# One attention and two gated layers on one core: fewer output transfers, another order of the first loads, and small matmuls and copies moved

## The chip, the cores and the metric

The kernel runs on one core of a Trainium2 chip. The metric is the time of one execution on the device in microseconds (us); lower is better. The five engines of the core are named as the profile names them: PE multiplies matrices (PEld is its weight load), DVE, ACT and POOL work on vectors, and SP issues transfers.

## The reference

Three stages follow one another. All are float32 in and out.

```python
batch, n_heads, seq, head_dim = (4, 8, 576, 64);  n_pack = 32
p_packed = sm_attn(p, k, v)                 # 32 packed queries per head look at 576 keys
out      = sm_attn(q, p_packed, p_packed)   # 576 queries per head look at the 32 packed rows
x = out.transpose(0, 2, 1, 3).reshape(2304, 512)

h = x @ w_in                                # w_in 512 x 2048
x = (max(h, 0) + log1p(exp(-abs(h)))) @ w_out          # w_out 2048 x 512

gate = 1 / (1 + exp(-(x @ w_gate)))         # w_gate, w_val 512 x 1536
y = (gate * (x @ w_val)) @ w_out2           # w_out2 1536 x 512
```

`sm_attn` is softmax attention with a scale of 1/8. The softmax of each row takes its own maximum off and divides by its sum.

## The kernel before

**Attention.** The work is cut into eight units: four batches, and in each two groups `g` of four heads (`attn_unit`, L330). A unit loads k, q and v as tiles of 128 partitions by 1152 numbers, 576 KB each. It goes through these steps:

- PE turns the unit's p (L333, out of `pall`, where the p of all units lies) and, in nine turns of 128x128, its k (L313); ACT copies the results out of PSUM as `pT` and `kT`.
- Eight small matmuls, `scores` (L326), make the first scores. DVE takes the maximum (L345), ACT the exponential with the sum (L348), DVE the reciprocal (L353) and the scaling of the 128x576 weights (L354), and turns them (L357).
- 72 small matmuls (L369) multiply the weights with v into two PSUM banks `pp`. Eight copies of 64x32 (L377, through the helper's L96 on ACT and L98 on DVE) bring the packed rows into `ppT`. `PPA = [1, 0]` puts the first four copies on ACT and the last four on DVE.
- Eight more `scores` matmuls give the scores of the 576 queries against the packed rows. A second softmax follows on DVE, ACT and POOL (L391 to L409), and its weights are split into a high and a low part `A2h` and `A2l` (L410, L411).

The trace counts each small float32 matmul twice: 8 of the program are x16 there, and 72 are x144.

**First layer.** The packed rows are multiplied into the first layer's weights ahead of time: `prep_wp` (L468) makes `Wp` out of `ppT` and a block of `w_in` (L480, eight small matmuls for one batch). `emit_h` (L498) multiplies `Wp` with the split softmax weights in three passes (L113 to L115), ACT makes the softplus (L509 to L511), and `emit_out1` (L528) multiplies with `w_out` (L537 to L540). All weights come in as pairs of 32-bit words that DVE turns into float32 with three instructions per half block (`convert`, L189, L194, L198).

**Second layer.** `emit_gv` (L786) makes gate and value by seven products (L113 to L115) and sums; `emit_out2` (L853) multiplies with the last weights (L859 to L861), adds into `acc` (L867), and after the last block sends each tile of 128 rows out.

**Loads.** SP issues nearly all transfers from one queue, in the order in which the scheduler put them, and stands at one that must wait. `load_kqv` (L229) takes k, q and v tiles in a fixed order and puts each in a free place: a slice of the big accumulator `xa`, or one of `NEXT = 2` own tiles. For units 6 and 7 only two slices and the own tiles are left. `done_kqv` (L240) loads two more when a tile has been used. `load_next` (L144) loads the next weight block into one of two `raw` buffers. `convert` calls it again at its end, so that a weight block is loaded when an earlier one has been converted. The p of all units is loaded by two transfers that ACT issues at the start (L275): each has 1024 runs of 256 bytes.

Each transfer holds one of eight semaphores for transfers until it has landed, and the next transfer with the same semaphore waits for it at issue.

**Order.** A scheduler orders the instructions of each engine by priority, which follows the order of the program, and by when it thinks that their inputs are there. Nothing in the kernel sets a priority. Semaphores are added afterwards; each engine runs its own list in order.

**Output.** `emit_out2` sends a tile of 128 rows as four transfers of 32 rows, 64 KB each (L875), because the rows of one tile belong to blocks that lie apart in the output.

```python
    while a < e:
        b, r = divmod(a, S)
        ee, cc = divmod(r // NR, NC)
        nc.sync.dma_start(outv[b, ee, cc], acc[a - t0 : a - t0 + NR])
        a += NR
```

Line numbers in the text are those of this kernel. The changed kernel's lines lie a few further on.

Of the kernel before, what the change touches and what calls it, by code (L numbers as in the profile page):

```python
# [11 lines left out]
I32 = mybir.dt.int32  # L12
AF = mybir.ActivationFunctionType
ALU = mybir.AluOpType
# [6 lines left out]
def attn_moe_moe_kernel(  # L21
# [24 lines left out]
    nc = tc.nc  # L46
    B, H, S, D = q.shape
    NK = p.shape[2]
    NT, DM = out.shape
    F1 = w_in.shape[1]  # L50
    F2 = w_gate.shape[1]
    P = 128
    NR = 32
    NC = S // NR // 2
# [4 lines left out]
    KD = DM // P  # L59
# [8 lines left out]
    L0 = 3  # L68
    GP = 7
    PO = ['k0', 'q0', 'k1', 'v0', 'q1', 'v1']  # L70
    XR = 0
    EARLY = [0]
    NCV = 5
    SC = float(D) ** -0.5
# [11 lines left out]
    xa = cst.tile([P, KD * NT], F32, name="xa")  # L86
# [4 lines left out]
    def bank1():  # L91
        return ps_o[-1].tile([P, 512], F32, tag="o", name="ps1")
# [26 lines left out]
    att = tc.alloc_tile_pool(name="att", bufs=1, side="right")  # L119
# [14 lines left out]
    for c in range(NCH1):  # L134
        order += [("in", c, f) for f in range(2)] + [("out", c, f) for f in range(2)]
        if c > ECS:
            n = -(-len(early) // (NCH1 - c))
# [6 lines left out]
    def load_next():  # L144
        if not waiting:
            return
        nm, c, f = key = waiting.popleft()
        if XR and key == ("out", 0, 0):

            t = xa[:, : 2 * DM].bitcast(I32).rearrange("p (n t) -> p n t", t=2)  # L150
        else:
            t = raw.tile([P, KD * P, 2], I32, tag="raw", name="raw_" + nm)
        a = c * CF + f * P
        if nm in ("out", "o2"):
            nc.sync.dma_start(t.rearrange("p n t -> p (n t)"), w32[nm][a : a + P, :])
        elif nm == "in":

            for g in range(2):
                nc.sync.dma_start(
                    t[64 * g : 64 * g + 64].rearrange("p (k n) t -> p k (n t)", k=KD),  # L160
                    w32[nm][256 * g : 256 * g + 256, 2 * a : 2 * (a + P)].rearrange(
                        "(k p) x -> p k x", p=64
                    ),
                )
        else:
            nc.sync.dma_start(
                t.rearrange("p (k n) t -> p k (n t)", k=KD),
                w32[nm][:, 2 * a : 2 * (a + P)].rearrange("(k p) x -> p k x", p=P),
            )
        raws[key] = t  # L170
# [41 lines left out]


    KQV = 2 * NC * D
    NEXT = 2
    own = [att.tile([P, KQV], F32, name=f"own{i}") for i in range(NEXT)]
    plan = deque((nm, u) for u in range(2 * B) for nm in "kqv")
    first = sorted((plan.popleft() for _ in range(6)), key=lambda x: PO.index(x[0] + str(x[1])))
# [47 lines left out]
    ppT = ph1.tile([P, B, H, NK], F32, name="ppT")  # L266
# [4 lines left out]


    pall = att.tile([P, 2 * B, 2, D], F32, name="pall")
    for i in range(2):
        nc.scalar.dma_start(  # L275
            pall[:, :, i], p.rearrange("b (g h) n d -> (h n) (b g) d", g=2)
        )

    NWORK = 7
    SPL = []  # L280
# [14 lines left out]
    LEFT = 1  # L295
    MARGIN = 0
    G0 = 2
    PPA = [1, 0]
    NW = 3
    GAP = 2  # L300
    LATE = 2
# [17 lines left out]

    def scores(lhsT, xT, to):  # L320

        for e in range(2):
            r = slice(64 * e, 64 * e + 64)
            for h in range(4):
                n = slice(NK * h, NK * h + NK)
                nc.tensor.matmul(  # L326
                    to[e][n], lhsT(r, h), xT[r, :, n], start=True, stop=True
                )

    def attn_unit(u):  # L330
        b, g = divmod(u, 2)
        px = bank1()
        nc.tensor.transpose(px[:, :P], pall[:, u].rearrange("p i d -> p (i d)"), ident)  # L333
        pT = att.tile([P, P], F32, tag="pT", bufs=2, name="pT")
        nc.scalar.activation(pT, px[:, :P], AF.Copy)
        kT = att.tile([P, NC, P], F32, tag="kT", bufs=1, name="kT")
        yield from turned(kqv.pop(("k", u)), kT)
        done_kqv("k", u)
        s1 = bank2()
        scores(  # L340
            lambda r, h: pT[r, NK * h : NK * h + NK], kT,
            [s1[:, e, :HS].rearrange("p (c r) -> p c r", r=NR) for e in range(2)],
        )
        mx = att.tile([P, 4], F32, tag="mx", bufs=2, name="mx")
        nc.vector.tensor_reduce(mx[:, 0:1], s1[:, :, :HS], op=ALU.max, axis=AX.XY)  # L345
        nc.vector.tensor_scalar(mx[:, 1:2], mx[:, 0:1], -SC, None, op0=ALU.mult)
        a1 = att.tile([P, S], F32, tag="a1", bufs=1, name="a1")
        nc.scalar.activation(  # L348
            a1.rearrange("p (a t) -> p a t", a=2), s1[:, :, :HS], AF.Exp,
            bias=mx[:, 1:2], scale=SC, accum_out=mx[:, 2:3],  # L350
        )
        nc.vector.tensor_scalar(mx[:, 2:3], mx[:, 2:3], 1e-9, None, op0=ALU.add)
        nc.vector.reciprocal(mx[:, 3:4], mx[:, 2:3])  # L353
        nc.vector.tensor_scalar(a1, a1, mx[:, 3:4], None, op0=ALU.mult)  # L354

        a1T = att.tile([P, 2 * NC, NK], F32, tag="a1T", bufs=2, name="a1T")
        nc.vector.transpose(a1T.rearrange("p c n -> p (c n)"), a1)  # L357
        yield
        qT = att.tile([P, NC, P], F32, tag="qT", bufs=2, name="qT")
        yield from turned(kqv.pop(("q", u)), qT)  # L360
        done_kqv("q", u)
        vt = kqv.pop(("v", u)).rearrange("p (c e d) -> p c e d", c=NC, e=2)

        pp = [bank1() for _ in range(2)]
        for e in range(2):
            for c in range(NC):
                for h in range(4):
                    r = slice(NR * h, NR * h + NR)
                    nc.tensor.matmul(  # L369
                        pp[h // 2][64 * (h % 2) : 64 * (h % 2) + 64, :NK],  # L370
                        vt[r, c, e, :], a1T[r, e * NC + c, :],
                        start=e == c == 0, stop=(e, c) == (1, NC - 1),
                    )
        done_kqv("v", u)
        for h in range(4):
            for x in range(2):
                copy(  # L377
                    PPA[h // 2], ppT[64 * x : 64 * x + 64, b, 4 * g + h, :],
                    pp[h // 2][64 * (h % 2) : 64 * (h % 2) + 64, :NK],
                )  # L380
        yield
        s2 = [bank1() for _ in range(2)]
        scores(
            lambda r, h: ppT[r, b, 4 * g + h, :], qT,
            [x[:, :HS].rearrange("p (c r) -> p c r", r=NR) for x in s2],
        )

        a2 = att.tile([P, 2 * NC, NK], F32, tag="a2", bufs=3, name="a2")
        m2 = att.tile([P, 2, 2 * NC], F32, tag="m2", bufs=3, name="m2")
        for e in range(2):  # L390
            nc.vector.transpose(  # L391
                a2[:, e * NC : (e + 1) * NC].rearrange("p c n -> p (c n)"), s2[e][:, :HS]
            )
        nc.vector.tensor_reduce(m2[:, 0], a2, op=ALU.max, axis=AX.X)
        nc.vector.tensor_tensor(
            a2, a2, m2[:, 0].unsqueeze(2).to_broadcast([P, 2 * NC, NK]), op=ALU.subtract
        )
        nc.scalar.activation(a2, a2, AF.Exp, scale=SC)
        yield
        nc.vector.tensor_reduce(m2[:, 1], a2, op=ALU.add, axis=AX.X)  # L400
        nc.vector.tensor_scalar(m2[:, 1], m2[:, 1], 1e-9, None, op0=ALU.add)
        nc.vector.reciprocal(m2[:, 1], m2[:, 1])
        nc.gpsimd.tensor_tensor(
            a2, a2, m2[:, 1].unsqueeze(2).to_broadcast([P, 2 * NC, NK]), op=ALU.mult
        )
        yield

        A2 = att.tile([P, S], F32, tag="A2", bufs=2, name="A2")
        nc.vector.transpose(A2, a2.rearrange("p c n -> p (c n)"))  # L409
        nc.scalar.activation(A2h[b][:, g], A2, AF.Copy)  # L410
        split_lo(nc.gpsimd, A2l[b][:, g], A2, A2h[b][:, g])  # L411
        yield
# [36 lines left out]
    w_in_f, wo_hl, Wp = {}, {}, {}  # L449
# [18 lines left out]
    def prep_wp(items):  # L468

        n = len(items)  # L470
# [2 lines left out]
            for y in "hl"  # L473
        )
        ps = [bank1().rearrange("p (i n) -> p i n", i=2)[:, :n] for _ in range(2)]
        for i, (b, c) in enumerate(items):
            for h in range(4):
                for t in range(2):
                    r = slice(64 * t, 64 * t + 64)
                    nc.tensor.matmul(  # L480
                        ps[t][NK * h : NK * h + NK, i], ppT[r, b, 4 * t + h, :],
                        w_in_f[c][r, h, :], start=True, stop=True,
                    )
            Wp[b, c] = (hi[:, i], lo[:, i])
        for t in range(2):
            if n == 1 or items[0][0] == items[1][0]:
# [207 lines left out]
    load_kqv(6)  # L694
    for _ in range(2):
        load_next()
    units.extend(range(2 * B))
    n = 0
    jobs.append(("win0", prep_win(0)))
# [153 lines left out]
    def emit_out2(ps, c, t):  # L853
# [15 lines left out]
        if c == NCH2 - 1:  # L869
            t0 = ps * HB * S + t * P  # L870
            a, e = t0, t0 + P
            while a < e:
                b, r = divmod(a, S)
                ee, cc = divmod(r // NR, NC)
                nc.sync.dma_start(outv[b, ee, cc], acc[a - t0 : a - t0 + NR])  # L875
                a += NR

    spread = [0.0]
    steps = [(ps, f) for ps in range(2) for f in range(NF)]
# [60 lines left out]
```

## Time and profile before

| | |
|---|---|
| three runs, median (range) | 885.8 us (882.84 to 887.54) |
| the profiled execution: its own time | 884.71 us |
| its span, first to last instruction | 882.9 us |
| mean granted clock of TensorE | 0.977 |
| busy share: PE, PEld | 93%, 86% |
| busy share: DVE, ACT, POOL | 71%, 43%, 51% |
| chain that ended last: PE, DVE | 77%, 11% |
| chain that ended last: ACT, transfers, issue, POOL | 3%, 3%, 3%, 2% |

The span runs from the first to the last instruction; the execution's own time is 1.8 us longer. PE is the engine that sets the pace: it is busy for 823.5 of the 882.9 us. The profile cuts the span into 40 slices of 22 us, and PE is at 9 tenths or more in nearly all of them but the first four and the last. The granted clock is that of the slices in tenths of full speed, where full is 2.4 GHz and half is 1.2 GHz.

### The profile page before, as it was taken

The page shows a single profiled execution, that of the slowest core. Times are in us where ns is not written, and L with a number is a line of the kernel's source. Part 1 is how long each engine was busy: PE and PEld are TensorE (multiplying, and loading weights), DVE is VectorE, ACT ScalarE, POOL GpSimd, SP SyncE. Part 2 cuts the span into 40 slices and gives each one's busy share as a digit, 9 for nine tenths or more (in the row PEclk, how much of TensorE's full clock was granted, in tenths as well). Part 3 has the DMA queues.
Part 4 walks back from the last instruction along what each step waited for, and adds up shares of the span by engine and source line. Part 5 has one row for each costly group of instructions (what it writes and reads, how often), then busy time and mean ns, then how long its engine had stood idle before and what let it go on. Part 6 is the DMA issues. An engine that isn't in the chain of part 4 may idle for free.

```text
span 882.9 us, 17370 instructions
## 1 busy us (share of the span) xinstructions
PE 823.5 (93%) x7040; PEld 755.4 (86%) x7040; DVE 626.0 (71%) x1057; ACT 376.3 (43%) x659; POOL 451.9 (51%) x420
## 2 busy tenths in 40 slices
PE   2976999999999999998999999999989999999995
PEld 1655788889989999998989999999869999999984
DVE  0757676778686577558898688897898656766763
ACT  1453666466555556666633331232342432322210
POOL 0043232366473555576469687886883633634400
PEclk9787999999999999998999999999999999999998
DMA  8644030123152223100055454645435312213004
GB/s 266 220 139 122 28 110 29 31 67 97 39 172 60 49 70 110 43 25 1 1 170 177 155 168 150 186 129 157 139 87 141 86 48 71 79 44 95 13 1 107
DMA packets 52480, 85.67 MB, mean 97 GB/s; under 512 B 6960, under 2 KB 30640, under 8 KB 52400
## 3 DMA queue, kind: packets, MB, share of 16 engines
q1 hardware_dynamic: 50320, 84.04, 32.5%
q8 instruction: 55, 0.90, 0.4%
q10 hardware_dynamic: 2080, 0.52, 0.3%
q14 instruction: 25, 0.20, 0.1%
HBM read 65.67 MB, written 18.87 MB: 96 GB/s over the span
## 4 chain that ended last, share of the span: by engine, by line
PE 77%; DVE 11%; ACT 3%; DMA 3%; issue 3%; POOL 2%; SPq 0%; POOLq 0%; ACTq 0%; DVEq 0%
PE bank L115 9%; PE bank L113 9%; PE bank L114 9%; PE ps L537 6%; PE ps L540 6%; PE ps L538 6%; PE ps L861 5%; PE ps L859 5%; PE ps L860 5%; PE ps L115 3%; PE ps L114 3%; PE ps L113 3%; DMA pall<-in_p_dram 2%; PE ps L369 2%; PE ps L313 2%
## 5 line engine op out<-in xcount | busy, mean ns | idle before, releaser
L113 PE MATMUL bank<-aop,BH 128*128 128x288 f32 x672 | 198.8, 296 | 3.7 <-DVE work L824 1.5
L114 PE MATMUL bank<-aop,BH 128*128 128x288 f32 x672 | 197.9, 295 | 1.0 <-DVE aop L101 0.9
L115 PE MATMUL bank<-aop,BL 128*128 128x288 f32 x672 | 198.6, 296 | 0.0
L101 POOL TENSOR_TENSOR ghl<-g,ghl 128x576 fp32r<-128x576 f32 x64 | 93.8, 1469 | 133.5 <-ACT ghl L108 133.5
L537 PE MATMUL ps<-ghl,woh 128*128 128x288 f32 x512 | 148.7, 305 | 6.0 <-DVE xa L545 3.6
L538 PE MATMUL ps<-ghl,wol 128*128 128x288 f32 x512 | 144.6, 297 | 0.0
L545 DVE TENSOR_TENSOR xa<-xa,ps 128x288 f32<-128x288 f32 x224 | 97.2, 448 | 59.0 <-PE ps L540 58.0
L113 PEld LDWEIGHTS bank<-aop,BH 128*128 128x128 f32 x672 | 126.2, 188 | 9.1 <-issue 1.4
L114 PEld LDWEIGHTS bank<-aop,BH 128*128 128x128 f32 x672 | 126.4, 188 | 5.1 <-DVE aop L101 1.6
L115 PEld LDWEIGHTS bank<-aop,BL 128*128 128x128 f32 x672 | 126.5, 188 | 0.0
L101 POOL TENSOR_TENSOR BL<-cv,BH 128x512 fp32r<-128x512 f32 (+1 forms) x96 | 116.8, 1231 | 11.3 <-ACT BH L108 10.2
L537 PEld LDWEIGHTS ps<-ghl,woh 128*128 128x128 f32 x512 | 97.4, 190 | 15.9 <-DVE xa L545 6.2
L540 PE MATMUL ps<-ghl,woh 128*128 128x288 f32 x512 | 110.6, 297 | 0.1
L538 PEld LDWEIGHTS ps<-ghl,wol 128*128 128x128 f32 x512 | 97.5, 190 | 0.5 <-issue 0.5
L812 DVE TENSOR_TENSOR work<-work,bank 128x576 f32<-128x576 f32 (+1 forms) x100 | 70.8, 725 | 29.8 <-PE bank L115 29.4
L859 PE MATMUL ps<-oh,gv 128*128 128x512 f32 x216 | 84.6, 392 | 1.3 <-DVE xa L867 0.8
L860 PE MATMUL ps<-ol,gv 128*128 128x512 f32 x216 | 84.8, 393 | 0.0
L861 PE MATMUL ps<-oh,gv 128*128 128x512 f32 x216 | 84.7, 393 | 0.0
L113 PE MATMUL ps<-A2h,wph 128*128 128x288 f32 x256 | 78.6, 309 | 6.3 <-ACT A2h L410 2.7
L540 PEld LDWEIGHTS ps<-ghl,woh 128*128 128x128 f32 x512 | 83.1, 189 | 0.4 <-POOL ghl L101 0.4
L867 DVE TENSOR_TENSOR xa<-xa,ps 128x512 f32<-128x512 f32 x90 | 61.5, 684 | 27.4 <-PE ps L861 26.9
L114 PE MATMUL ps<-A2l,wph 128*128 128x288 f32 x256 | 77.7, 304 | 1.9 <-POOL A2l L101 1.9
(115 smaller groups left out, 1576.0 us busy)
## 6 DMA issues: line engine op xcount, KB each, us to landing
cv<-B SPq DMA_DIRECT2D x52, 256.0 KB, 2.7
B<-cv SPq DMA_DIRECT2D x48, 256.0 KB, 4.2
raw_in<-in_moe_w_in_dram SPq DMA_DIRECT2D x32, 256.0 KB, 4.1
raw_out<-in_moe_w_out_dram SPq DMA_DIRECT2D x16, 512.0 KB, 3.7
raw_g<-in_moe_w_gate_dram SPq DMA_DIRECT2D x12, 512.0 KB, 4.0
raw_v<-in_moe_w_val_dram SPq DMA_DIRECT2D x12, 512.0 KB, 4.4
raw_o<-in_moe_w_out_dram SPq DMA_DIRECT2D x12, 512.0 KB, 4.2
out_dram<-xa SPq DMA_DIRECT2D x72, 64.0 KB, 1.7
```

The lines of the kernel that those rows point to most:

```text
L101: eng.tensor_tensor(lo, x, hi.bitcast(F32), op=ALU.subtract)
L113: nc.tensor.matmul(ps, wh, xh, start=first, stop=False)
L114: nc.tensor.matmul(ps, wh, xl, start=False, stop=False)
L115: nc.tensor.matmul(ps, wl, xh, start=False, stop=last)
L537: nc.tensor.matmul(out_, wh[:, ms], gh[:, f], start=f == 0, stop=False)
L538: nc.tensor.matmul(out_, wl[:, ms], gh[:, f], start=False, stop=False)
L540: nc.tensor.matmul(out_, wo_hl[c, f][0][:, ms], gl[:, f], start=False, stop=f == 1)
L545: nc.vector.tensor_tensor(dst, dst, out_, op=ALU.add)
L812: nc.vector.tensor_tensor(to, x, y, op=ALU.add)
L859: nc.tensor.matmul(bank, gh[:, ts_], oh, start=f == 0, stop=False)
L860: nc.tensor.matmul(bank, gh[:, ts_], ol, start=False, stop=False)
L861: nc.tensor.matmul(bank, gl[:, ts_], oh, start=False, stop=f == 1)
```

## The change

It has seven parts.

1. A tile's output rows that lie one after the other in `outv` go out in one transfer of up to four blocks of 32 rows; a half of the tokens takes 12 transfers instead of 36.
2. The p of units 0 and 1 is loaded by four small transfers that ACT issues first (128 runs of 256 bytes each); that of units 2 to 7 by two transfers on SP's queue, after the first four of `w_in`.
3. The first two blocks of `w_out` get tiles of their own (`raw_first`), and are loaded at the start too.
4. To make room for these, k, q and v have one own tile instead of two (`NEXT = 1`).
5. The blocks of small matmuls (`scores`, the product with v, and those of `prep_wp`) are put 300 places ahead in priority.
6. All eight copies into `ppT` run on ACT.
7. The scaling of the first softmax's weights runs on ACT instead of DVE.

```diff
-    XR = 0
+    FIRST = [("out", 0, 0), ("out", 0, 1)]
...
-        if XR and key == ("out", 0, 0):
-
-            t = xa[:, : 2 * DM].bitcast(I32).rearrange("p (n t) -> p n t", t=2)
+        if key in FIRST:
+            t = att.tile([P, KD * P, 2], I32, name=f"raw_first{c}{f}")
...
-    NEXT = 2
+    NEXT = 1
...
-    for i in range(2):
-        nc.scalar.dma_start(
-            pall[:, :, i], p.rearrange("b (g h) n d -> (h n) (b g) d", g=2)
-        )
+
+    def load_p(eng, a, e):
+        src = p.rearrange("b (g h) n d -> (h n) (b g) d", g=2)
+        for i in range(2):
+            eng.dma_start(pall[:, a:e, i], src[:, a:e])
+
+    load_p(nc.scalar, 0, 1)
+    load_p(nc.scalar, 1, 2)
...
-    PPA = [1, 0]
+    PRIO = 300
...
     def scores(lhsT, xT, to):
-        for e in range(2):
...
+        with tc.high_priority(PRIO):
+            for e in range(2):
...
-        nc.vector.tensor_scalar(a1, a1, mx[:, 3:4], None, op0=ALU.mult)
+        nc.scalar.activation(a1, a1, AF.Copy, scale=mx[:, 3:4])
...
-                    PPA[h // 2], ppT[64 * x : 64 * x + 64, b, 4 * g + h, :],
+                    True, ppT[64 * x : 64 * x + 64, b, 4 * g + h, :],
...
     load_kqv(6)
+    for _ in range(2):
+        load_next()
+    load_p(nc.sync, 2, 2 * B)
     for _ in range(2):
         load_next()
...
                 ee, cc = divmod(r // NR, NC)
-                nc.sync.dma_start(outv[b, ee, cc], acc[a - t0 : a - t0 + NR])
-                a += NR
+                n = min((e - a) // NR, NC - cc)
+                nc.sync.dma_start(outv[b, ee, cc : cc + n], acc[a - t0 : a - t0 + n * NR])
+                a += n * NR
```

The product with v and the matmuls of `prep_wp` are put under the same `tc.high_priority(PRIO)` as `scores`.

The change moves instructions at three places that matter below.

SP's queue from its start, before (k, q and v go to `xa` or `own`, `raw_in` is a half block of `w_in`, `raw_out` one of `w_out`):

```order
L236 DMA xa<-in_k_dram 128x1152
L236 DMA xa<-in_q_dram 128x1152
L236 DMA xa<-in_k_dram 128x1152
L236 DMA xa<-in_v_dram 128x1152
L236 DMA xa<-in_q_dram 128x1152
L236 DMA xa<-in_v_dram 128x1152
L159 DMA raw_in<-in_moe_w_in_dram 64x4x256 x4
L236 DMA xa<-in_k_dram 128x1152
L236 DMA xa<-in_q_dram 128x1152
L155 DMA raw_out<-in_moe_w_out_dram 128x1024 x2
```

and with the change, from the same place:

```order
L235 DMA xa<-in_v_dram 128x1152
L158 DMA raw_in<-in_moe_w_in_dram 64x4x256 x4
L277 DMA pall<-in_p_dram 128x6x64 x2
L154 DMA raw_first_120<-in_moe_w_out_dram 128x1024
L154 DMA raw_first_122<-in_moe_w_out_dram 128x1024
L235 DMA xa<-in_k_dram 128x1152
L235 DMA xa<-in_q_dram 128x1152
L158 DMA raw_in<-in_moe_w_in_dram 64x4x256 x4
```

The first six transfers are the same. Then the rest of p and both halves of the first `w_out` block come ahead of unit 2's k and q, and the second block of `w_in` follows right behind them; before, it came as the eighteenth row, behind `raw_out` and nine tiles of k, q and v.

PE from its start, with the change (`kT` of unit 0 is `ps_129` to `ps_139`; `ps_149` is the first piece of unit 1's k):

```order
L337 MATMUL ps_124<-ident,pall 128x128
L316 MATMUL ps_129<-ident,xa 128x128 x3
L316 MATMUL ps_134<-ident,xa 128x128 x3
L316 MATMUL ps_139<-ident,xa 128x128 x3
L337 MATMUL ps_144<-ident,pall 128x128
L316 MATMUL ps_149<-ident,xa 128x128 x2
L330 MATMUL ps_158<-kT,pT 32x288 x8
```

Unit 0's first scores (the last row) stand behind the turn of unit 1's p and two turns of unit 1's k. Before, the same seven rows stand there with x3 in the sixth.

PE at unit 0's second scores (`ps_321` and `ps_322`, after the product with v), before:

```order
L313 MATMUL ps_316<-ident,xa 128x128 x3
L326 MATMUL ps_321<-qT,ppT 32x288 x3
L326 MATMUL ps_322<-qT,ppT 32x288 x2
L313 MATMUL ps_338<-ident,xa 128x128
L326 MATMUL ps_322<-qT,ppT 32x288
L313 MATMUL ps_338<-ident,xa 128x128 x2
L326 MATMUL ps_321<-qT,ppT 32x288
L369 MATMUL ps_348<-a1T,xa 64x32 x15
L326 MATMUL ps_322<-qT,ppT 32x288
```

and with the change (`ps_329` and `ps_330`):

```order
L316 MATMUL ps_324<-ident,xa 128x128 x3
L330 MATMUL ps_329<-qT,ppT 32x288 x4
L330 MATMUL ps_330<-qT,ppT 32x288 x4
L316 MATMUL ps_346<-ident,xa 128x128
L374 MATMUL ps_356<-a1T,xa 64x32 x17
```

The eight matmuls stand together now, behind three turns of q. Over the whole program the product with v stands in 9 pieces instead of 11 (8 would be whole), the scores in 15 instead of 21, and the order is otherwise much the same.

## Rows read from the trace of the kernel before

**Rows 1.** Stages: length, busy us (instructions) of PE, PEld, DVE, ACT, POOL; clock, DMA share, GB/s.

```profile
0.00:17.40 17.40, 0.00 (x0) 0.03 (x1) 0.00 (x0) 1.28 (x1) 0.70 (x6) 1.00 0.92 278
...
33.00:45.00 12.00, 11.68 (x181) 7.68 (x178) 7.97 (x20) 4.51 (x14) 2.05 (x2) 0.57 0.96 346
...
54.00:65.00 11.00, 9.62 (x184) 7.79 (x185) 3.24 (x4) 5.67 (x12) 3.54 (x4) 0.69 0.51 157
65.00:74.00 9.00, 2.68 (x26) 0.97 (x32) 8.75 (x23) 2.55 (x6) 1.42 (x1) 0.83 0.17 54
74.00:81.00 7.00, 6.06 (x36) 4.81 (x21) 5.64 (x10) 1.33 (x4) 2.43 (x2) 0.50 0.50 147
81.00:860.00 779.00, 760.91 (x6296) 711.44 (x6296) 575.45 (x955) 346.40 (x590) 437.21 (x404) 1.00 0.30 87
860.00:882.90 22.90, 12.82 (x54) 9.47 (x52) 8.30 (x13) 0.68 (x1) 0.00 (x0) 0.86 0.40 103
```

**Rows 2.** Timeline of the start: start us, us, engine, line, operation, count [idle before <-releaser].

```profile
0.74 0.40 SPq L236 DMA_DIRECT2D xa<-in_k_dram  x1
0.76 1.08 ACTq L275 DMA_DIRECT2D pall<-in_p_dram  x2
...
4.89 13.00 SPq L159 DMA_DIRECT2D raw_in<-in_moe_w_in_dram  x4
...
17.41 0.44 PE L333 MATMUL ps<-ident,pall 128*128 128x128 f32 x1 [17.41 <-DMA pall<-in_p_dram]
...
20.55 1.21 PE L326 MATMUL ps<-kT,pT 64*32 64x288 f32 x16
```

**Rows 3.** Waits: engine, line <- waited for: us in total, times, longest us.

```profile
SPq L159 <- DMA pall<-in_p_dram: 9.9, 2, 8.7
...
PE ps L480 <- DVE w_in L198: 5.9, 1, 5.9
```

**Rows 4.** L236's first six transfers, issue to landing.

```profile
DMA to landing us min/median/max: 4.1/8.4/11.9
```

**Rows 5.** Transfers 3 to 4.5 us: ACT's queue: packets, MB, share of 16 engines.

```profile
q10 hardware_dynamic: 535, 0.14, 40.1%
```

**Rows 6.** Transfers 6 to 8 us, then 16 to 18 us.

```profile
DMA packets 401, 0.81 MB, mean 403 GB/s; under 512 B 238, under 2 KB 238, under 8 KB 401
...
DMA packets 613, 0.45 MB, mean 226 GB/s; under 512 B 222, under 2 KB 612, under 8 KB 613
```

**Rows 7.** Timeline: unit 2's first turn of k, and SP's later weight loads.

```profile
28.69 4.03 SPq L155 DMA_DIRECT2D raw_out<-in_moe_w_out_dram  x2
...
38.91 0.85 PE L313 MATMUL ps<-ident,xa 128*128 128x128 f32 x3
...
44.10 9.56 SPq L159 DMA_DIRECT2D raw_in<-in_moe_w_in_dram  x4
```

**Rows 8.** Groups: line, engine, operation, count | busy us, mean ns | idle before, releaser.

```profile
L354 DVE TENSOR_SCALAR a<-a,mx 128x576 f32<-128x576 f32 x8 | 4.2, 519 | 0.2
L98 DVE COPY ppT<-ps 64x32 f32<-64x32 f32 x32 | 6.0, 187 | 5.0 <-PE ps L369 4.5
...
L96 ACT ACTIVATE ppT<-ps 64x32 f32<-64x32 f32 x24 | 4.5, 189 | 1.4 <-PE ps L369 1.2
L348 ACT ACTIVATE a<-ps,mx 128x576 f32<-128x576 f32 x5 | 3.7, 743 | 1.7 <-DVE mx L346 1.7
```

**Rows 9.** The end: timeline, then line L875: issue ns min/median/max, first and last start; landing.

```profile
863.45 17.12 SPq L875 DMA_DIRECT2D out_dram<-xa  x36
...
873.33 0.69 DVE L867 TENSOR_TENSOR xa<-xa,ps 128x512 f32<-128x512 f32 x1 [0.67 <-PE ps L861]
...
L875 SPq DMA_DIRECT2D out_dram<-xa x72: 315/424/582, 658.0 to 880.1; - x72
...
DMA to landing us min/median/max: 1.6/1.7/2.6
```

**Rows 10.** Line L655, transfers of 128 KB and 256 KB to HBM: issue to landing.

```profile
DMA to landing us min/median/max: 1.7/4.0/5.8
```

More of the change, by code (lines that the diff above doesn't have):

```diff
@@ L320, in scores @@
     def scores(lhsT, xT, to):
-        for e in range(2):
[L323 to L328, printed above, removed]
+        with tc.high_priority(PRIO):
+            for e in range(2):
+                r = slice(64 * e, 64 * e + 64)
+                for h in range(4):
+                    n = slice(NK * h, NK * h + NK)
+                    nc.tensor.matmul(
+                        to[e][n], lhsT(r, h), xT[r, :, n], start=True, stop=True
+                    )
     def attn_unit(u):
@@ L364, in attn_unit @@
         pp = [bank1() for _ in range(2)]
[L365 to L373, printed above, removed]
+        with tc.high_priority(PRIO):
+            for e in range(2):
+                for c in range(NC):
+                    for h in range(4):
+                        r = slice(NR * h, NR * h + NR)
+                        nc.tensor.matmul(
+                            pp[h // 2][64 * (h % 2) : 64 * (h % 2) + 64, :NK],
+                            vt[r, c, e, :], a1T[r, e * NC + c, :],
+                            start=e == c == 0, stop=(e, c) == (1, NC - 1),
+                        )
         done_kqv("v", u)
@@ L475, in prep_wp @@
         ps = [bank1().rearrange("p (i n) -> p i n", i=2)[:, :n] for _ in range(2)]
-        for i, (b, c) in enumerate(items):
[L477 to L483, printed above, removed]
+        with tc.high_priority(PRIO):
+            for i, (b, c) in enumerate(items):
+                for h in range(4):
+                    for t in range(2):
+                        r = slice(64 * t, 64 * t + 64)
+                        nc.tensor.matmul(
+                            ps[t][NK * h : NK * h + NK, i], ppT[r, b, 4 * t + h, :],
+                            w_in_f[c][r, h, :], start=True, stop=True,
+                        )
+        for i, (b, c) in enumerate(items):
             Wp[b, c] = (hi[:, i], lo[:, i])
```

## The prediction

> **What bounds the kernel now.** I read the stages first, then the timeline of the start, the waits, and the end. From 81 us to 860 us PE is busy for 760.9 of 779 us at full clock [rows 1]. An edit that saves work on DVE, ACT or SP there gives back at most the 18 us left, so the change is decided in the first 81 us and the last 23. At the start PE does nothing for 17.4 us [rows 1]: its first matmul turns the p of unit 0, and what ends its wait is the p transfer [rows 2]. From 65 to 74 us PE is busy for only 2.7 of 9 us, while DVE is busy for 8.8 [rows 1]; the longest wait there, 5.9 us, is for DVE's last conversion of the second `w_in` block [rows 3]. PE runs at half clock (1.2 GHz) for parts of 33 to 81 us [rows 1], after thin stretches. At the end DVE's last sum is done at 873.33 + 0.69 = 874.0 us, but SP is still issuing: 36 output transfers from 863.45 us, one each 0.42 to 0.48 us, the last at 880.1 us [rows 9].
>
> **The change part by part.** The sum is made against the profiled execution, 884.7 us, which is 1.1 us below the median of the three runs.
>
> *p of units 0 and 1 first.* The wait for p goes; what is late next is the data. Unit 0's k is issued at 0.74 us [rows 2] and lands 4.1 us later, if the shortest of the first six landings is its own [rows 4]: 4.8 us. The four p transfers are 512 runs; in 1.5 us ACT's queue moved 535 of them beside SP's [rows 5]. So PE can start at about 5.5 us. But unit 0's scores stand behind two turns of unit 1's k, the third tile. Two more tiles of 0.59 MB at 403 GB/s [rows 6] put it at 4.8 + 2.9 = 7.7 us, some 0.6 us more for the p in between. I take 8.5 us for the scores, against 20.55 us before [rows 2]: **12.0 us earlier**. Bounds: if unit 1's k, issued about a microsecond after unit 0's, lands only after the median 8.4 us [rows 4], the scores come at about 10.5 us, 10 us earlier; if it lands at 6 us, 14 us earlier.
>
> Does the gain hold through the next steps? The six tiles, the first `w_in` (1.05 MB at the 226 GB/s of its stretch, 4.6 us [rows 6]), the other 1536 runs of p (at 0.40 x 1.5 us per 535, 1.7 us [rows 5]), `raw_first` (1.05 MB, 3.0 us at 346 GB/s [rows 1]) and unit 2's k come through by about 11.1 + 4.6 + 1.7 + 3.0 + 1.5 = 22 us. Unit 2's first turn of k stood at 38.9 us [rows 7] and would stand at 27. So it does not wait; if the loads take 5 us longer, this cover is gone, and unit 1's second scores, which stand behind it, wait too. The eight transfer semaphores also hold less: SP's `w_in` issues stood 9.9 us for p's [rows 3], and nothing as slow as p is in flight now.
>
> *`w_out` in tiles of its own, second `w_in` block earlier.* Before, SP issued the second `w_in` block from 44.1 us, in 9.6 us, after the `w_out` issues at 28.7 us had given the `raw` buffers back [rows 7]. Now it needs only the first `w_in` block converted, which comes 12 us earlier as well. DVE can then convert it before 65 us; it is busy for 3.2 of the 11 us from 54 to 65 us [rows 1]. At most this gives the 6.3 idle us of 65 to 74 us, and half of the 6.06 busy us that follow at half clock [rows 1], 3.0 us. At least it gives nothing, since DVE has attention work in the same stretch, which then ends last. I take the middle, **5 us**.
>
> *Scaling and copies on ACT.* The scaling takes 0.52 us on DVE; ACT's nearest row, the exponential over the same 576 columns, takes 0.74 us [rows 8]. That is 0.22 us longer in the chain of each unit. The eight copies take 8 x 0.19 = 1.5 us on one engine instead of 0.75 us on each of two [rows 8]. If the whole difference stood on the path, it would be 8 x (0.22 + 0.75) = 7.8 us. Against it, the 32 DVE copies waited their turn between conversions, and DVE loses 4.2 + 6.0 us of work [rows 8] in the stretch where it is fullest. I take 0; bounds 7.8 us lost and, if half of DVE's relief counts, 5 us won. The Trainium skill speaks against both moves: the page "ScalarE: Activation LUTs", section "Rules for kernel authors", gives multiplications to VectorE, and "TensorEngine Tiling (Array Packing)", section "PSUM Bottleneck", says to empty PSUM with both engines. By those rules the sum would be 7.8 us worse; the trace agrees on the price of the scaling, and no row yet shows which engine is late in the changed kernel.
>
> *Priority.* No matmul is added or taken away, and most blocks already stood whole. Where the scores of unit 0 wait for copies one by one, a whole block waits once. Between the product with v and unit 0's second scores there are three turns both times, so the cover is the same. I take 0, bounds 3 us either way.
>
> *One own tile less.* Units 6 and 7 have three places instead of four, so unit 7's k comes once unit 6's has been turned. A late tile costs about one landing, 4.1 us at least [rows 4]; I take 0, since a second unit starts only when the first has done seven of its steps (`GP = 7`, L435).
>
> *Output.* The last tile is one transfer of 256 KB, issued at 874.1 us. It moves four times the bytes of the 64 KB transfers, which landed in 1.7 us [rows 9]; the 128 and 256 KB transfers to HBM landed in 1.7 to 5.8 us, median 4.0 [rows 10], five in a row. I take 2.7 us, nearer to the first because only the tile before it can be in the way. What followed the last landing stays: 882.9 - 880.1 - 1.7 = 1.1 us. End: 877.9 us, **5.0 us earlier**; with 1.7 and 4.0 us it is 6.0 and 3.7. The first half's transfers, at 658 us [rows 9], lie where PE sets the pace; 0.
>
> Sum: 884.7 - 12.0 - 5.0 - 5.0 = 862.7, say **863 us**.
>
> **The rivals.**
>
> *Start and end alone.* The second `w_in` block is not what counts at 65 us: DVE's attention work or ACT's longer chain ends last. For it: DVE is busy for 8.75 of 9 us there [rows 1]. Against: the wait that ends last is the conversion's [rows 3]. 884.7 - 12 - 5 = 868; with ACT's full 7.8 us, 875.5. That last is what the two rules above would do here.
>
> *The start's gain is lost on the way.* If the steps up to 81 us are held by loads or DVE and not by the start, the later stages do not move, and only the end's 5 us remain: 879.7. For it: the transfer engines are busy for 0.92 of the first 17.4 us [rows 1]. Against: 27 us of later loads fit in 22, as worked out above.
>
> *The blocks put ahead hold PE: slower.* With priority, `scores` go to the head of PE's list, and PE stands there until ACT has made all eight copies, 1.5 us, behind whatever ACT has queued. With five activations of 0.74 us ahead [rows 8] that is 5.2 us in each of eight units, 42 us, against 17 saved: 910. It decides from (17 + 4.4) / 8 = 2.7 us per unit on (4.4 us being half a per cent). Against: ACT is busy for under half of 81 to 860 us [rows 1], and the covers in the order are as before.
>
> *The full clock holds.* If the denser start keeps PE at full clock, half of the time at half clock comes back. The 11.7 busy us of 33 to 45 us at a mean of 0.57 alone would give about 5 us [rows 1]: 858.
>
> **How the numbers follow.** Forecast 0.50, start and end alone 0.28, full clock 0.11, the start's gain lost 0.07, slower 0.04. A measurement of this kernel can tell about 0.5% (4.4 us) from no change. The forecast's own range is 856 to 868: start -14 to -10, middle -9 to 0, end -6.0 to -3.7, not all at one side. The range for all reaches to 875 for ACT's price and to 852 for the clock: **852 to 875**. Left out are the loss of the start's gain, the slower case and the tails of the rest, about 2 in 10. Faster by over 0.5% (below 881.4) holds in all cases but the slower one and a third of the lost start: **0.92**; within 0.5% **0.05**; slower **0.03**.
>
> **What would show it.** PE's first matmul at 5 to 6 us and unit 0's scores at 8 to 9 us; the main matmuls (L113 to L115) starting 10 us or more earlier than before; no wait of several us of the `prep_wp` matmuls on DVE; 12 output transfers in each half and an end some 4 us behind DVE's last sum. I am wrong if PE waits in the first 30 us for tiles of k or for the rest of p, if waits of PE on ACT's `ppT` copies come to more than a few us, or if from 81 us on PE's idle time grows.

## The result and the profile after

The changed kernel takes 895.1 us (median of 7 runs, 890.44 to 897.95); on the same chip the kernel before takes 883.51 us (7 runs, 882.44 to 887.54). The ratio is 1.011 with a 95% interval of 1.008 to 1.0145: **slower** by 1.1%, about 10 us, outside the range forecast (852 to 875) and on the other side. The profiled execution of the change takes 895.1 us with a span of 893.3 us, against 884.71 and 882.9 us. In the changed kernel L277 loads p, L316, L330, L374 and L486 are turns, scores, product with v and `prep_wp`, and L877 and L887 the last sum and the output.

The start came within its bounds. The timeline of the changed kernel (columns as in [rows 2]):

```profile
0.77 2.24 ACTq L277 DMA_DIRECT2D pall<-in_p_dram  x4
...
6.62 0.45 PE L337 MATMUL ps<-ident,pall 128*128 128x128 f32 x1 [6.62 <-DMA pall<-in_p_dram]
...
9.79 0.45 PE L337 MATMUL ps<-ident,pall 128*128 128x128 f32 x1 [0.80 <-DMA pall<-in_p_dram]
...
10.59 1.21 PE L330 MATMUL ps<-kT,pT 64*32 64x288 f32 x16
```

PE starts 10.8 us earlier and unit 0's scores come 10.0 us earlier than in [rows 2]. What PE waits for is still p: unit 0's until 6.62 us, and for unit 1's turn, at 9.79 us, another 0.80 us. It waits for no tile of k there. But the stages, in the columns of [rows 1], show what became of it. First the changed kernel, then the one stretch of the kernel before that [rows 1] does not have:

```profile
0.00:17.40 17.40, 8.65 (x86) 6.32 (x89) 2.43 (x7) 7.68 (x16) 0.70 (x6) 1.00 0.96 282
17.40:33.00 15.60, 13.03 (x303) 9.29 (x295) 10.81 (x23) 4.47 (x14) 0.00 (x0) 0.60 1.08 321
33.00:45.00 12.00, 7.57 (x61) 3.77 (x61) 7.26 (x14) 6.82 (x21) 5.46 (x5) 0.64 0.47 171
...
65.00:74.00 9.00, 9.00 (x107) 7.16 (x102) 5.41 (x13) 3.21 (x7) 0.00 (x0) 0.62 0.00 0
...
81.00:860.00 779.00, 758.13 (x6106) 705.34 (x6104) 566.16 (x926) 347.41 (x598) 434.02 (x402) 1.00 0.29 87
860.00:893.30 33.30, 11.78 (x51) 8.99 (x49) 6.87 (x11) 0.00 (x0) 0.00 (x0) 0.71 0.23 71
```

```profile
17.40:33.00 15.60, 14.26 (x246) 9.95 (x246) 9.03 (x23) 8.22 (x22) 0.00 (x0) 1.00 0.39 128
```

From 17.4 to 33 us PE had full clock (2.4 GHz) before; now the mean granted clock is 0.60, so it is at 1.2 GHz for most of that stretch. By the records of the granted clock, PE stood at half clock from 33.4 to 43.7, 53.9 to 60.8 and 71.0 to 81.2 us before, 27.3 us of the first 200. Now it does from 20.7 to 37.7, 41.1 to 54.8, 61.6 to 71.9 and 88.9 to 92.3 us: 44.4 us. Half a microsecond is the most that a microsecond at half clock can cost, so the 17.1 us more are worth at most 8.6 us. For the same 7040 matmuls PE is busy for 831.0 us in the page of the changed kernel, against 823.5. From 65 to 74 us PE is now busy all the time (9.00 of 9 us, 2.7 before): the wait for the second `w_in` block in [rows 3] is gone. The mean clock is 0.62 there.

Following the same instruction through both traces gives the account (us from the span's start; the lead is before less after; a `Wp` block is a group of `prep_wp`'s matmuls):

| start of (or end, where said) | before | after | lead |
|---|---|---|---|
| first matmul | 17.4 | 6.6 | 10.8 |
| unit 0's first scores | 20.6 | 10.6 | 10.0 |
| first `Wp` block | 43.1 | 37.8 | 5.3 |
| second `Wp` block | 73.8 | 64.5 | 9.3 |
| first sum into `xa` | 101.2 | 92.6 | 8.6 |
| fourth `Wp` block | 132.8 | 127.6 | 5.2 |
| second layer's first sum into `acc` | 518.5 | 515.1 | 3.4 |
| 40th sum into `acc` | 660.2 | 656.8 | 3.4 |
| 46th | 732.1 | 730.6 | 1.4 |
| end of the last one | 874.0 | 872.6 | 1.4 |
| end of the span | 882.9 | 893.3 | -10.4 |

The lead goes in four places. 4.7 us go between unit 0's scores and the first `Wp` block, and PE stands at half clock from 20.7 to 37.7 us. 4.0 us come back by the second `Wp` block, where the wait for `w_in` is gone. 5.2 us go between the first sum into `xa` and 515 us; the changed kernel is at full clock from 92.3 us on, so this is not half clock there, and only the experiment on the priority below says something of it. 2.0 us go between the 40th and the 46th sum, and 11.8 us at the end (20.7 us from the last sum to the end of the span, 8.9 before). The end is the largest. The changed kernel's timeline of it, then its output line (issue ns min/median/max, first and last start):

```profile
862.01 19.70 SPq L887 DMA_DIRECT2D out_dram<-xa  x12
...
871.90 0.69 DVE L877 TENSOR_TENSOR xa<-xa,ps 128x512 f32<-128x512 f32 x1 [0.67 <-PE ps L871]
```

```profile
L887 SPq DMA_DIRECT2D out_dram<-xa x24: 349/843/5068, 654.6 to 880.1; - x24
```

There are 12 issues in place of 36 in [rows 9], as forecast, but SP needs 19.7 us for them instead of 17.1. The line holds both halves: the issue of 5.07 us is one of the first half, and it waits for the semaphore of an earlier transfer. In the second half the longest takes 3.21 us (from 868.2 us), and the trace shows no semaphore that it waits for; what holds it is not shown. What the transfers do then is in the view of the transfer engines, from 878 to 893 us in 40 slices (busy tenths of 16 engines, GB/s, then the queue's packets, MB and share):

```profile
DMA  2223453232222222222222222222111111100000
GB/s 104 93 109 120 120 126 104 76 87 66 60 71 60 55 93 82 98 104 104 98 104 104 98 104 109 93 98 82 49 49 55 55 44 55 55 22 27 11 0 0
...
q1 hardware_dynamic: 592, 1.14, 22.4%
```

Nothing else runs, yet the transfers move 100 GB/s, then 50, then 25, in steps, with 2 tenths, 1 tenth and less of the 16 engines busy. The kernel before moved 108 to 168 GB/s with four tenths and more busy while it sent the same half, and what it had to send was gone 1.7 us after each issue [rows 9]. The steps read as four engines at 25 GB/s each, then two, then one.

A merged transfer writes n blocks of 32 x 512, and n is at most 4. The trace does not name the engine of a packet, but the count of packets tells how many engines a transfer is spread over. First the changed kernel's second half with its issues, then that of the kernel before (36 transfers of 64 KB; one packet is another queue's):

```profile
DMA packets 1218, 2.36 MB, mean 61 GB/s; under 512 B 66, under 2 KB 66, under 8 KB 1218
out_dram<-xa SPq DMA_DIRECT2D x6, 256.0 KB
out_dram<-xa SPq DMA_DIRECT2D x2, 192.0 KB
out_dram<-xa SPq DMA_DIRECT2D x2, 128.0 KB
out_dram<-xa SPq DMA_DIRECT2D x2, 64.0 KB
```

```profile
DMA packets 1729, 2.37 MB, mean 108 GB/s; under 512 B 576, under 2 KB 576, under 8 KB 1728
```

Both send 1152 rows of 2 KB; the rest are packets under 512 B. Before, these are 576 = 36 x 16. In the change they are 66 = 6 x 4 + 2 x 3 + 2 x 2 + 2 x 16. This is what one small packet for each engine gives, if n merged blocks use n engines and a single block of 32 rows uses sixteen. The Trainium skill states such a rule in the page "DMA: Bandwidth & Descriptors", section "Why a DMA increments its semaphore by 16 and not by 1": the number of engines is the largest up to 16 that divides the slowest dimension (of those that are not 1) of both access patterns. For 4 x 32 x 512 that is 4, for 32 x 512 it is 16; the counts of 66 and 576 agree with both.

The 36 blocks of a half are 36 x 64 KB = 2.36 MB, and at 100 GB/s that takes 23.6 us, against 31.3 us from the first issue at 862.0 us to the end: the output is now bound by the transfers. From the last sum's end at 872.6 us on, nothing else is left to do. The first half's output does the same on SP's queue (changed kernel, then before):

```profile
654.64 18.40 SPq L887 DMA_DIRECT2D out_dram<-xa  x11
...
675.44 21.54 SPq L681 DMA_DIRECT2D cv<-B  x9
```

```profile
658.03 17.27 SPq L875 DMA_DIRECT2D out_dram<-xa  x36
675.40 20.89 SPq L674 DMA_DIRECT2D cv<-B  x10
```

The outputs start 3.4 us earlier and yet the weights' loads behind them start at the same 675.4 us: between the 40th and the 46th sum, which need the later weights, the 2.0 us go.

### The profile page after: what moved, and what is told of

It reads as the page before. It is cut to its first block, busy times and chain, and to the rows that moved or that the text cites. A ratio compares the mean times of both kernels' runs of the same rounds, so it can differ in the third digit from the quotient of the medians.

```text
span 893.3 us, 17332 instructions
## 1 busy us (share of the span) xinstructions
PE 831.0 (93%) x7040; PEld 758.5 (85%) x7040; DVE 613.5 (69%) x1017; ACT 387.5 (43%) x699; POOL 451.5 (51%) x420
## 4 chain that ended last, share of the span: by engine, by line
PE 71%; DVE 13%; ACT 6%; DMA 2%; issue 2%; POOL 2%; ACTq 0%; SPq 0%; DVEq 0%; POOLq 0%
PE bank L113 9%; PE bank L115 9%; PE bank L114 9%; PE ps L871 5%; PE ps L869 5%; PE ps L870 5%; PE ps L545 5%; PE ps L544 5%; PE ps L547 5%; PE ps L114 3%; PE ps L113 3%; PE ps L115 3%; DVE aop L101 2%; DVE xa L552 2%; PE ps L486 2%
## 5 line engine op out<-in xcount | busy, mean ns | idle before, releaser
L877 DVE TENSOR_TENSOR xa<-xa,ps 128x512 f32<-128x512 f32 x90 | 61.5, 683 | 27.3 <-PE ps L871 26.9
```

## The experiments

All ratios are against the kernel before, run beside the experiment on the same chip. There were three groups, each on a chip of its own, with medians of 883.65 us for the kernel before (the output and the start alone), 883.0 us (fillers, moves, first priority run, two queues with p first) and 884.67 us (the rest). Between groups the ratios compare better than the times, so both are given where they differ. The stages and leads come from one profiled execution of each kernel.

**The output, undone and alone.** First, the change with its blocks of 32 rows back:

```diff
-                n = min((e - a) // NR, NC - cc)
-                nc.sync.dma_start(outv[b, ee, cc : cc + n], acc[a - t0 : a - t0 + n * NR])
-                a += n * NR
+                nc.sync.dma_start(outv[b, ee, cc], acc[a - t0 : a - t0 + NR])
+                a += NR
```

> The change with the output sent in blocks of 32 rows again, all else kept. Theory: the merged transfers use only as many of the 16 transfer engines as they have blocks (4, 3 or 2); with single blocks the end comes about 9 us after DVE's last sum, as before, and the 2.0 us that the first half's outputs cost between 655 and 690 us go too. Time about 880 us, 15 below the change and 3 to 4 below the kernel before. Rival: the slow end comes from the scheduler's other order or from the colder clock; then the time stays near 893.

Measured: 881.64 us (10 runs), ratio 0.9954 [0.9931, 0.9977]. That is 13.5 us below the change. The rival, a time that stays near 893 us, is out. The 40th to the 46th sum take 71.9 us again, as before (73.9 in the change), and the end follows the last sum by 8.7 us.

Then the merged transfers alone, the same edit the other way round in the kernel before:

> The kernel before with the merged output transfers alone. Theory: about 12 us more at the end and 2 us after the first half, 897 us, with the transfer engines near a quarter of their time busy in the last 20 us. Rival (the merged form needs the other edits to be slow): 884 us or less.

Measured: 897.38 us (4 runs), ratio 1.015 [1.0124, 1.0176]. Here too the 40th to the 46th sum take 2 us longer (74.0 us), and the end follows the last sum by 20.8 us. The last 15 us of its span look like those of the change:

```profile
DMA  2224443332213122222222222221111111100000
GB/s 104 104 98 131 137 109 98 93 76 71 60 76 60 66 87 82 104 98 109 98 98 104 98 104 104 98 98 76 49 49 55 49 49 55 49 27 27 11 0 0
...
q1 hardware_dynamic: 596, 1.15, 22.2%
```

So the merged output by itself costs about 13 us, from both sides, and turns a small gain into a loss.

**Is the end bound by SP's issues, then?** The change with 32-row blocks, of which ACT issues about every other one (16 of 36) in the second half; the diff is against that kernel with one queue:

```diff
+                eng = nc.scalar if ps and cc % 2 else nc.sync
-                nc.sync.dma_start(outv[b, ee, cc], acc[a - t0 : a - t0 + NR])
+                eng.dma_start(outv[b, ee, cc], acc[a - t0 : a - t0 + NR])
```

> The change with blocks of 32 rows, and in the second half every other block issued by ACT, which is idle there. Theory: 16 engines per transfer, and the issue time halved: four blocks of a tile take about 0.9 us of issue on each queue against 1.36 us between tiles, so that the end comes 4 to 5 us after DVE's last sum: about 875 us. Rival: HBM writes, not issue, hold the end back; then as with one queue, 880 us.

Measured: 878.86 us (5 runs), 0.9942 [0.9922, 0.9963]. The end follows the last sum by 4.2 us instead of 8.7. So the reading of [rows 9], that SP's issue time bounds the end, was right, and sharing the issues between two queues takes 4.5 us off the distance that the merging was to shorten. In the time less arrives: 2.8 us by the medians, 1.1 us by the ratios, whose intervals overlap; 875 us was expected. It is the distance in the traces that tells.

**The start alone.** The kernel before, with p of units 0 and 1 loaded first and the rest on SP, and nothing else (two own tiles, no `raw_first`):

```diff
-    for i in range(2):
-        nc.scalar.dma_start(
-            pall[:, :, i], p.rearrange("b (g h) n d -> (h n) (b g) d", g=2)
-        )
...
+    load_p(nc.scalar, 0, 1)
+    load_p(nc.scalar, 1, 2)
...
     for _ in range(2):
         load_next()
+    load_p(nc.sync, 2, 2 * B)
```

> The kernel before with the p of units 0 and 1 loaded first alone. PE starts near 6.6 us instead of 17.4. Theory: most of these 10.8 us are lost again by 200 us because the earlier start of the sparse stage only lengthens its stretch at half clock; time about 879 to 881 us. Rival: the gain is lost to the other edits (ACT's copies, priority, the own tile); then 873 to 875 us.

Measured: 878.25 us (7 runs), 0.9941 [0.9919, 0.9964], a little below the 879 to 881 expected: about half of the 10.8 us is lost, not most of it. The lead over the kernel before is 9.6 us at unit 0's scores and 3.1 at the third `Wp` block (92.4 us, 95.5 before), and stays near 4 from there. Half clock takes 44.4 us of the first 200, as in the change, and PE's wait for the second `w_in` block is still there:

```profile
PE ps L484 <- DVE w_in L198: 6.6, 1, 6.6
```

**Is it the clock that eats the start's gain?** The same kernel, with 13 more matmuls in each of units 0 to 3: 3 ahead of the first scores, 5 ahead of the product with v, 5 ahead of the second scores. Each writes 128x512 into a bank that the next matmuls overwrite, so PE does more, and the result is the same. (`identR` is the identity matrix in another 32-bit form, made once by POOL.)

```diff
+    def fill(u, bank, n):
+        if u > 3:
+            return
+        for _ in range(n):
+            nc.tensor.matmul(
+                bank.rearrange("p (a n) -> p a n", a=4), identR,
+                identR.unsqueeze(1).to_broadcast([P, 4, P]), start=True, stop=True,
+            )
...
         s1 = bank2()
+        fill(u, s1[:, 0], 3)
...
         pp = [bank1() for _ in range(2)]
+        fill(u, pp[0], 5)
...
         s2 = [bank1() for _ in range(2)]
+        fill(u, s2[0], 5)
```

> As e5_p_first, with 13 matmuls of 128x128 by 512 columns without use in each of the first four attention units, ahead of its two blocks of scores and its product with v, in banks that these overwrite. They cost 52 x 0.23 = 12 us of PE at full clock, partly in its waits. Clock theory: the time at half clock in the first 100 us falls from 44 us to well under 30, and the time falls by 2 to 5 us, to 873 to 876, in spite of the added work. Rival (the lost gain has to do with chains on DVE and ACT, not with the clock): the added work only costs, 880 to 888 us.

Measured: 872.06 us (4 runs), 0.9869 [0.9837, 0.9901]: 6.2 us faster with 52 more matmuls, a little more than the 2 to 5 us expected. The stages (columns of [rows 1]) without and with the fillers:

```profile
17.40:33.00 15.60, 13.27 (x254) 7.91 (x248) 8.35 (x20) 3.16 (x9) 0.00 (x0) 0.68 0.94 330
33.00:45.00 12.00, 10.77 (x108) 5.66 (x103) 8.27 (x19) 4.76 (x14) 2.56 (x2) 0.50 0.35 122
```

```profile
17.40:33.00 15.60, 12.76 (x334) 9.46 (x333) 10.72 (x29) 5.17 (x16) 0.18 (x1) 0.89 0.95 340
33.00:45.00 12.00, 8.58 (x81) 5.13 (x80) 10.77 (x19) 5.72 (x13) 7.20 (x5) 0.86 0.65 194
```

The granted clock rises from 0.68 and 0.50 to 0.89 and 0.86, and half clock in the first 200 us falls from 44.4 to 13.7 us. In the whole kernel PE is busy for 822.3 us, 7.1 less than without the fillers, although it has more to do. The lead over the kernel before, 8.0 us at unit 0's scores, is 10.6 at the third `Wp` block (84.9 us), where it was 3.1 without. This is the direct evidence that much of the start's gain goes into matmuls at half clock. Not all of the 6.2 us need be the clock: PE's wait for the second `w_in` block falls too, from 6.6 to 3.3 us.

**The moves to ACT.** The change with 32-row blocks, and with the scaling and half of the copies back on DVE:

```diff
-        nc.scalar.activation(a1, a1, AF.Copy, scale=mx[:, 3:4])
+        nc.vector.tensor_scalar(a1, a1, mx[:, 3:4], None, op0=ALU.mult)
...
-                    True, ppT[64 * x : 64 * x + 64, b, 4 * g + h, :],
+                    h < 2, ppT[64 * x : 64 * x + 64, b, 4 * g + h, :],
```

> As e1_single_out, with the scaling and half of the copies back on DVE. e1 is 3.4 us slower than p first alone (881.6 against 878.3). If ACT's longer chain is the reason, this gives about 878 us; if it is the priority, the places or the clock, it stays at 881 to 882.

Measured: 878.56 us (10 runs), 0.9946 [0.9923, 0.9969]. That is 3.1 us below the kernel with the moves by the medians and 0.7 by the ratios, and the intervals overlap: no gain of the moves is seen, and whether they cost about 3 us stays open.

**The priority.** The change with 32-row blocks and each `with tc.high_priority(PRIO):` taken out (three places):

> As e1_single_out, without the priority for the small matmuls. If the blocks put ahead hold PE, about 878 us; if not, 881 to 882.

Measured: 873.31 us (4 runs), 0.9889 [0.9854, 0.9923]. The priority costs 8.3 us by the medians and 5.7 by the ratios, and the intervals lie apart. The two kernels stand level at 62 us (the same second scores start at 62.88 and 62.73 us). From 60 to 80 us, with the priority and without:

```profile
60.00:80.00 20.00, 18.48 (x255) 13.27 (x255) 10.97 (x25) 10.33 (x31) 4.30 (x4) 0.66 0.16 40
```

```profile
60.00:80.00 20.00, 17.84 (x285) 13.11 (x286) 13.23 (x28) 12.12 (x35) 8.26 (x6) 0.83 0.32 89
```

With it PE is busy for longer and starts fewer matmuls (255 against 285), at a clock of 0.66 instead of 0.83: half clock lasts to 74.4 us instead of 66.7. The third `Wp` block then comes at 88.5 us with the priority and 85.3 without, the fourth at 129.7 and 124.5, the second layer's first product at 447.4 and 439.8. So 3.2 us are lost up to the third block and 4.4 us behind it.

In the page PE is busy for 832.9 against 826.1 us with the same matmuls: 6.8 of the 7.6 us between the two profiled executions (883.22 and 875.61 us) are PE's own time and not waits. The clock is only a part of that. With the priority PE stands at half clock for 47.8 us up to 860 us, without it for 41.0 (34.1 in the first 200 us, 6.9 later): 6.8 us more, worth 3.4 at most. What the rest is, the runs do not show; much of it lies behind the third block, where the change too loses its lead at full clock.

**The priority on the kernel with p first**, on the scores and the product with v:

```diff
+        with tc.high_priority(300):
+            for e in range(2):
```

> The kernel before with p of units 0 and 1 first (878.25 us by itself) and with the priority on the scores and on the product with v, nothing else. If the priority alone costs the 8 us that taking it out of the change gave: 886 us. If it costs only together with the copies on ACT (PE stands at the block until ACT has made all eight copies): within 2 us of 878.25.

Measured: 882.38 us (10 runs), 0.998 [0.9959, 1.0001], 4.1 us above the kernel with p first alone by the medians, 3.4 by the ratios; the two intervals just touch. Neither of the two times expected came out. The priority gains nothing here either, and whether its cost depends on what stands around it is not settled by so small a difference.

**Two queues with p first alone**, as a check that the parts add:

> As e5_p_first, with every other output block of the second half issued by ACT. The two gains lie at the two ends and should add: 878.3 less 2.8 (e1 against e4), 875.5 us. If issue is no longer what ends last, less.

Measured: 875.15 us (7 runs), 0.9907 [0.9876, 0.9939]: 3.1 us below p first alone, where 2.8 was expected from the change. The intervals overlap, so this agrees with a sum of the two gains and does not prove it.

**All that helped, together.** Three kernels, all with fillers and two output queues: the change without the priority; the change with it; and the kernel before with p first.

> The change without the priority, with 32-row output blocks (every other one of the second half issued by ACT) and with the 13 filler matmuls (128x128x512, overwritten by what follows, so nothing of the computation is left out) in each of units 0 to 3. If the clock and the end are two separate costs, their gains add: 873.3 us without priority and with one output queue, less 3 us for the second queue and less some 3 us for the clock (that kernel spent 34.1 us at half clock in the first 200 us, and 13.7 us are reached with fillers; 0.5 x 20 us = 10 at most, of which the added matmuls take part back): 867 us, half clock under 20 us, ratio 0.981. If the filler only helped because p-first alone was short of PE work, 870 us or more.

> The same as the kernel before it in this call, but with the priority of the change. Theory A: the priority costs 8 us because the order that it makes leaves PE in thin stretches at half clock (47.8 us at half clock with it, 34.1 without); with fillers the clock is the same in both, and the two kernels differ by less than 2.5 us. Theory B: the priority costs by its order itself (PE stands at a block whose inputs are late, with fillers or without): 6 to 8 us slower than its neighbour.

> The kernel before with p of units 0 and 1 first, with the fillers, and with every other output block of the second half issued by ACT: no raw_first, no moves to ACT, no priority. The two gains add: 872.1 us less 3.1 us for the second queue is 869 us. If the four parts of the change that this kernel does not have are worth anything once the clock is full, it is slower than the kernel with them and without priority (867 us expected); if they are worth nothing, the two agree within 1.5 us.

Measured: 868.36 us, 0.9815 [0.979, 0.9839] without the priority; 883.97 us, 0.9997 [0.9976, 1.0017] with it; 864.54 us, **0.9774 [0.9751, 0.9797]**, with p first, fillers and two queues alone. The first came as expected (867 us), with 10.2 us at half clock in the first 200. The last is the fastest of all, 20 us below the kernel before and some 30 below the change. It beats the neighbour that also has `raw_first`, one own tile and the moves to ACT by 3.8 us (the intervals touch, the runs of the two do not overlap): once the clock and the output are right, those parts together gain nothing and seem to cost a little.

The kernel with priority and fillers was no clean test: half clock was not the same (30.7 us in the first 200, 10.2 without the priority). Its 15.6 us over its neighbour are more than the 6 to 8 expected by the theory that the order costs, and the groups of the first 130 us say why (with the priority, then without; columns as in [rows 8]):

```profile
L387 PE MATMUL ps<-a1T,xa 32*64 32x32 f32 x720 | 25.9, 240 | 0.2 <-DVE a1T L373 0.2
```

```profile
L387 PE MATMUL ps<-a1T,xa 32*64 32x32 f32 x720 | 12.0, 218 | 1.1 <-issue 1.1
```

The same 720 matmuls of the product with v keep PE busy for 25.9 instead of 12.0 us. The fillers hold the first of the two banks `pp`, so with the priority the scheduler seems to have put all matmuls of one bank first and then all of the other, where in program order they alternate by pairs. (The trace shows two runs of 72 with fillers between them; it does not name the bank.) Timelines of the two kernels:

```profile
18.47 2.29 PE L387 MATMUL ps<-a1T,xa 32*64 32x32 f32 x72 [0.19 <-DVE a1T L373]
...
21.70 4.05 PE L387 MATMUL ps<-a1T,xa 32*64 32x32 f32 x72
```

```profile
19.14 2.30 PE L387 MATMUL ps<-a1T,xa 32*64 32x32 f32 x144
```

72 in a row take as long as 144 that alternate, and at half clock (from 21.4 us) it takes 4.05 us. In the changed kernel itself the product with v is not split in this way: in the first 130 us it takes 15.8 us in the change, 16.3 with 32-row blocks, and 15.8 with these and without the priority. So that cost belongs to this experiment; what the priority does in the change beyond the clock is not settled by it.

## Why the prediction was wrong

- **The output step failed, and it alone turned the sign.** It read "The last tile is one transfer of 256 KB, issued at 874.1 us" and "I take 2.7 us": a landing taken from transfers of 64 KB that use sixteen engines, with "only the tile before it can be in the way". SP came to that issue only at 880.1 us, and the span ended 13.2 us later, since nearly all of the half's 2.36 MB queue on the same few transfer engines. The term was -5.0; it measured +11.8 at the end and +2.0 after the first half. The first half's 0 failed for the same reason: its outputs hold SP and so the loads of the weights behind them. The bounds were of the size of a transfer, but what mattered was its shape. No rival held this; the slower rival (blocks ahead that hold PE) has another mechanism.
- **The start step came within its bounds, in part by another way, and was not kept.** Forecast -12.0, measured -10.0 at unit 0's scores, the bound for a late tile of unit 1's k. No tile of k was late: "The wait for p goes" is what did not hold, PE stood for p until 6.62 us (5.5 forecast) and again for 0.80 us, so that the number met that bound by luck. The question "Does the gain hold through the next steps?" was asked of loads and buffers only, and those held: PE's waits for k come to 0.7 us in the first 130 us. What came next was the clock, 27.3 to 44.4 us at half clock; the text had the clock only as a gain (the rival of the full clock) and put half clock "after thin stretches". The fillers show the loss directly.
- **The middle step was right in its wait, and near its size.** PE's 5.9 us on DVE's conversion are gone with `raw_first` and stay (6.6 us) with p first alone. Between the first and the second `Wp` block the change makes up 4.0 us, against 5.0 forecast; with 32-row blocks it is 2.2 and with p first alone 1.7, so the part of `raw_first` in it is not sharp.
- **The moves to ACT, taken at 0**, lie inside the bounds of -5 to +7.8: a cost of 0.7 us by the ratios or 3.1 by the medians, with intervals that overlap. The 7.8 us of the two rules cited are not seen.
- **The priority, taken at 0 with 3 us either way**: a cost of 5.7 to 8.3 us, outside. The cover was judged from the order's blocks alone, and PE's waits on ACT's copies did stay small (2.4 us ahead of the second scores); the rival's mechanism is not what took the time. Up to half of it is the clock; the rest stays open.
- **One own tile less** at 0: PE's 0.7 us for k tiles speak for it; no run tests it alone.
- **A sign that the prediction named was there**: from 81 to 860 us PE's idle time grew, from 18.1 to 20.9 us.

## What to carry to other kernels

Fewer and larger transfers win only if each is still spread over many transfer engines: look at the slowest dimension of both sides before merging, count the small packets, and read busy share and GB/s of the queue together. Where issues bound an end, a second queue shortens it. Time won by an earlier start can be lost to PE's clock: follow the lead at many later instructions, since it can come back and go again, and compare PE's busy time and its microseconds at half clock for the same matmuls before calling the one the cause of the other.

## What was not expected of the hardware

- PE falls to half clock while it has small matmuls to do and is busy for most of the time: in the change it is busy for 8.53 of the 10 us up to 20 us, all at full clock, and falls at 20.7 us; in the kernel before it is busy for 14.26 of the 15.6 us up to 33 us and falls at 33.4 us. With 52 matmuls of no use among them the kernel was 6.2 us faster.
- Of the product with v, 72 matmuls in a row of the kernel with priority and fillers took 2.29 us and 144 of its neighbour 2.30 us, both at full clock. That the first stay in one bank and the second alternate between two is read from the program.
- Merged transfers of two to four blocks moved 100 GB/s with nothing beside them, and what was left at the end 50 and 25 GB/s; 32-row blocks from two queues moved up to 313 GB/s.
